# A fused mixer and MLP on one core: the first two input tiles alone, v's weights on another queue, and a new order of the steps

## The chip, the cores and the metric

The kernel runs on one core of one Trainium2 chip. A core has five engines that run their own instruction streams and meet at semaphores: TensorE (matrix products, PE in the profile, with PEld for its weight loads), VectorE (DVE), ScalarE (ACT), GpSimd (POOL) and SyncE (SP), which here only issues DMAs. The metric is the time of one execution in microseconds (us), median of three runs.

## The reference

`A_x` is 2048 rows of 512 numbers, all inputs are bfloat16.

```python
x  = A_x                                   # [1, 2048, 512]
xn = layernorm(x)                          # no learned scale or bias
# A: attention over 8 earlier positions, 2 apart; 32 heads of 16
q, k, v = split(xn @ wqkv)                 # wqkv [512, 1536]
logits  = sum_d q[s] * k[s - 2*u], u = 0..7, / 4; -1e9 where s < 2*u
s  = (softmax(logits) weighted sum of v[s - 2*u]) @ wo
# B: two MLP halves with shifts along the rows
h  = gelu(layernorm(xn) @ w1)
hs = concat(h's four quarters, shifted by +1, -1, +2, -2 rows) @ w2
x1 = xn + hs
g  = silu(x1 + gelu(layernorm(x1) @ w3) @ w4)   # w3 [512, 1376]
out = x + s * g
```

## The kernel before

The 2048 rows are worked on in four chunks of 512 rows (`c` 0 to 3), each of four tiles of 128 rows (`i` 0 to 15, in pairs `k` 0 to 7). The program is a list of small steps, `ORDER`, written out in a string. Each word of it is a step with its arguments: `qk.0.3.2` is step `qk` for chunk 0, column block 3, into PSUM bank 2. A step issues one to thirty-odd instructions on one engine. Each engine takes its instructions in the order of the list and waits at semaphores for what it reads, so the list sets the order on every engine at once, but not the times. Letters in a DMA step name the issuing queue: `s` SyncE, `a` ScalarE, `g` GpSimd.

The head of the list. `ldxp` (L221) loads a pair of x tiles, `ldv` (L234) half of v's weights (two of the four row blocks of the contraction), `ldw1` (L241) half of w1, `ldqk` (L228) the weights of q or k; all on SyncE's queue. `c_warm` (L275) clears a tile on VectorE, and `warmup` (L321) multiplies it with itself on TensorE, ten times 512 columns wide and later eight times 128 wide, while nothing else is there to do. `c_zero` (L288 to 290) writes 14 rows of zeros ahead of v in DRAM and clears the halo of `hT`, on GpSimd. For chunk 0, `st` (L333, L334) takes mean and variance on VectorE, `sq0` (L338) the square root on ScalarE, `nm0` (L344, L345) normalises on VectorE, `tr0` (L356) transposes on TensorE and `ev0h` or `ev0a` (L364, L360) moves the transposed tile to SBUF on ScalarE. For later chunks `xT` does it with a transposing DMA.

The matrix steps on TensorE: `v` (L471), `w1` (L496), `qk` (L443), `w2` (L611), `w3` (L668), `w4` (L685) and `wo` (L768); each takes four matmuls of 512 columns, `w4` eleven. `lg` (L543) sums products of q and k over a head, `ws` (L729) sums weighted v. Six PSUM banks (0 to 5) take the results, and a double one those of `lg`; the last argument of a step is its bank, and a bank is free again when ScalarE or VectorE has read it. ScalarE evicts `ev` (v, L481), `eqk` (L452), `eh` (gelu of w1, L507), `eg` (gelu of w3, L677). VectorE does `pw` (products of q and shifted k, L530), `smx`, `sms`, `smn` (softmax), `xa` (adds w2's result, L618), `st3s` (statistics of x1, L622), `nm3` (normalises x1, L645), `vp` (weights times v, L716), `ya`, `sg`.

DMAs in the middle: `sv` (L489, GpSimd) stores an evicted v tile to DRAM, out of a ring of three buffers `vt`; `vl` (L710, SyncE) reads v back with the shifts; `x1Tr` (L655), `hTr`, `oTr`, `tE` are transposing DMAs on SyncE. `x1Tr(k)` gives half a chunk of x1 transposed, which `w3` reads. `pre` copies x to the output, and `soa` (L835, GpSimd) adds a finished tile to it.

The tail: for tiles 12 to 15, `oTp` (L756) transposes on TensorE and `eoT` (L762) evicts; `wo` follows, then `ge` (L782), `gb` (L786), `fav` (L819) finish a tile; tile 15 goes in two halves, `woh`, `sgh`, `favh`, `soh`.

Of the kernel before, what the change touches and what calls it, by code (L numbers as in the profile page):

```python
# [9 lines left out]
ALU = mybir.AluOpType  # L10
# [18 lines left out]
qk.1.6.3 xa.1 nb.7 qk.1.0.2 nb.6 st3s.1 eqk.1.6 hTr.3 rr.4 xa.0 ldw3.s.0 st3s.0 eqk.1.5 pw.0.6
nm.13 nm.12 nm.15 qk.1.7.0 qk.1.3.4 w2.2.5 w1.9.3 w1.8.1 eh.9 eh.8 xa.2 rr.7 hTr.4 rr.5 rq.0  # L30
w1.10.5 pw.0.7 r3.0 v.8.3 eh.10 st3s.2 nm.14 w2.3.1 nm3.0 nm3.1 eqk.1.3 w2.5.5 ev.8 qk.2.0.4
xa.3 st3s.3 eqk.1.7 eqk.1.0 xT.6 lg.0.3 rq.1 kh.2 xa.5 lg.0.2 r3.1 w2.4.2 smx.0 ldw3.s.1 sv.8
xT.7 x1Tr.0 v.10.5 qk.2.4.0 w2.6.1 eqk.2.4 nm3.3 xa.4 ex.0 w2.7.3 w1.11.2 xa.6 st3s.6 nm3.2 xa.7
qk.2.5.1 eqk.2.0 x1Tr.1 eh.11 ev.10 sv.10 rr.6 v.9.0 v.11.3 w1.13.4 eqk.2.5 ev.9 hTr.5 qk.2.7.2
w1.15.1 eqk.2.7 w1.12.0 vl.s.2.0 vl.s.0.0 ldw4.s.2 qk.2.2.2 vl.s.3.1 eh.12 pw.1.0 st3s.4 st3s.7
st3s.5 v.12.5 eqk.2.2 pw.1.3 sms.0 eh.13 v.13.0 w3.0.6.4 ev.11 hTr.6 rq.2 qk.2.1.3 pw.1.2 r3.2
sv.9 eg.0.6 eqk.2.1 ldwo.s.3 smn.0 rq.3 pw.1.1 r3.3 w3.0.1.2 qk.2.3.4 w3.0.10.3 nm3.4 eqk.2.3
tE.0 eh.15 eg.0.10 ev.13 eg.0.1 lg.1.1 lg.1.0 pw.1.7 w2.8.1 w1.14.0 w3.0.0.2 eh.14 w3.0.2.3
hTr.7 qk.2.6.0 eqk.2.6 eg.0.0 w2.10.4 nm3.6 vl.s.0.1 nm3.7 x1Tr.3 vl.s.1.0 pw.1.5 xa.8 pw.1.4
nm3.5 pw.1.6 w2.11.1 xa.10 w3.0.8.2 xa.11 qk.3.1.4 st3s.11 eg.0.8 ev.12 w2.14.1 lg.1.2 st3s.10  # L40
sv.12 lg.1.3 eqk.3.1 w2.12.4 sv.11 st3s.8 eg.0.2 smx.1 w2.9.3 ldw4.s.1 x1Tr.2 xa.9 w2.15.5 xa.14
w3.0.3.2 w3.0.9.3 xa.12 pw.2.2 qk.3.2.1 qk.3.0.4 w2.13.0 st3s.9 eqk.3.2 eqk.3.0 eg.0.3 vl.s.9.1
ldw4.s.0 rq.4 xa.15 vl.s.9.0 vl.s.3.0 ldwo.s.2 pre.s.2 qk.3.3.1 w3.0.5.2 st3s.12 qk.3.4.5 eg.0.5
pw.2.3 eqk.3.3 qk.3.5.4 st3s.14 pw.2.4 xa.13 pw.2.1 rq.5 st3s.15 v.15.1 eqk.3.5 v.14.2 ev.15
eqk.3.4 w3.1.1.0 w3.0.4.5 vp.0 st3s.13 rq.6 pw.2.0 r3.4 nm3.9 w3.0.7.1 eg.0.4 ev.14 eg.0.9
eg.0.7 ex.1 qk.3.7.4 w3.1.0.2 eg.1.0 sv.14 r3.5 nm3.10 rq.7 nm3.11 x1Tr.5 w3.1.8.1 vl.s.2.1
# [27 lines left out]
def kernel(  # L74
# [116 lines left out]
    def xtile(i):  # L191
        return x_c[i // TPC][:, i % TPC, :]
# [71 lines left out]
    def ldwo(q, a):  # L264
# [5 lines left out]
        qs[q].dma_start(out=wo_sb[32 * a : 32 * a + 32, :, :], in_=src)  # L270


    @step
    def c_warm():
        nc.vector.memset(warm[:], 0.0)  # L275

    @step
    def c_ident():
        make_identity(nc, ident[:])

    @step
    def c_small():
# [1 line left out]
        nc.gpsimd.memset(mhalf[:], -0.5)  # L284

    @step
    def c_zero():
        nc.gpsimd.dma_start(out=v_dram[0:PADK, :], in_=warm[0:PADK, :])  # L288
# [586 lines left out]
```

## Time and profile before

| what | value |
|---|---|
| median of 3 runs | 190.42 us (190.27 to 190.52) |
| the profiled execution | 190.75 us |
| its span, first to last instruction | 189.0 us |
| TensorE busy | 182.8 us, 97% |
| VectorE busy | 165.1 us, 87% |
| ScalarE busy | 112.8 us, 60% |
| GpSimd busy | 42.7 us, 23% |
| granted TensorE clock, mean | 0.996 |
| DMA | 39.25 MB, mean 208 GB/s |

The profile is of one execution. Rows of the time line read: start, duration, engine, line of the kernel, operation, what it writes `<-` what it reads, how often, and in brackets how long the engine had been idle and what ended that. `SPq` and `ACTq` rows are the issuing of a DMA, not its transfer. The chain of waits follows back from the last instruction, at each step to what released it.

### The profile page before, as it was taken

How to read it: one execution, taken by the hardware profiler on the slowest of the kernel's cores; microseconds unless marked ns; L12 is line 12 of the kernel's file. 1: busy time of each engine (PE TensorE's matmuls, PEld its weight loads, DVE VectorE, ACT ScalarE, POOL GpSimd, SP SyncE). 2: the span in 40 equal slices, each digit the busy share in tenths (PEclk: the TensorE clock that was granted, in tenths of full speed). 3: DMA queues.
4: the chain of work that ended last, by engine and by line, in shares of the span. 5: the costliest groups of instructions: out<-in, count | busy, mean ns of one | idle time of the engine just before them, and what ended most of it. 6: DMA issues, size and time to landing. Idle time of an engine off the chain costs nothing.

```text
span 189.0 us, 3685 instructions
## 1 busy us (share of the span) xinstructions
PE 182.8 (97%) x1430; PEld 87.0 (46%) x1430; DVE 165.1 (87%) x270; ACT 112.8 (60%) x189; POOL 42.7 (23%) x70
## 2 busy tenths in 40 slices
PE   7999999999999999999999999999999999999990
PEld 2444445445444545444444555444455444444450
DVE  2694797997999899999989998999999999989554
ACT  3578669666595636045941465969529664742780
POOL 4157156423010702010450000000050003005350
PEclk9999999999999999999999999999999999999998
DMA  5994986987969929965989929999974999796783
GB/s 164 315 352 115 199 248 141 194 238 137 233 120 286 278 64 224 222 87 190 399 162 361 274 57 134 254 401 277 189 190 95 254 335 238 210 254 106 88 106 116
DMA packets 47842, 39.25 MB, mean 208 GB/s; under 512 B 35251, under 2 KB 41889, under 8 KB 47777
## 3 DMA queue, kind: packets, MB, share of 16 engines
q1 hardware_dynamic: 45008, 35.14, 74.6%
q0 software_dynamic: 2528, 3.69, 10.9%
q8 instruction: 11, 0.18, 0.4%
q10 hardware_dynamic: 288, 0.20, 0.3%
q14 instruction: 7, 0.05, 0.1%
HBM read 26.41 MB, written 5.78 MB: 170 GB/s over the span
## 4 chain that ended last, share of the span: by engine, by line
PE 85%; DMA 4%; DVE 4%; issue 2%; POOL 2%; SPq 1%; ACT 1%; POOLq 0%
PE mm L668 20%; PE mm L685 18%; PE mm L443 15%; PE mm L611 8%; PE mm L496 7%; PE mm L471 6%; PE lg L543 4%; PE mm L768 4%; DMA xc<-in_A_x_dram 3%; PE mm L729 3%; POOL out_dram L835 2%; DMA out_dram<-xr 1%; DVE st L333 1%; DVE xr L775 1%; DVE xr L786 1%
## 5 line engine op out<-in xcount | busy, mean ns | idle before, releaser
L530 DVE TENSOR_TENSOR pw<-qT,kT 128x2048 bf16<-128x2048 bf16 x32 | 38.3, 1214 | 3.4 <-PE lg L543 2.4
L668 PE MATMUL mm<-x1T,w_sb 128*128 128x512 bf16 (+1 forms) x176 | 40.9, 379 | 0.0
L685 PE MATMUL mm<-w_sb,h 128*128 128x512 bf16 (+1 forms) x176 | 39.4, 379 | 0.0
L677 ACT ACTIVATE h<-mm 128x512 bf16<-128x512 f32 (+1 forms) x44 | 23.9, 602 | 23.3 <-PE mm L668 17.6
L716 DVE TENSOR_TENSOR vs<-vs,att 128x4096 bf16<-128x4096 bf16 x16 | 36.2, 2285 | 0.0
L443 PE MATMUL mm<-xnT,wqk_sb 128*128 128x512 bf16 x128 | 30.6, 379 | 0.0
L835 POOL DMA_DIRECT2D out_dram<-xr x12 | 11.0, 1117 | 74.0 <-DVE xr L775 74.0
L668 PEld LDWEIGHTS <-w_sb 128*128 128x128 bf16 (+1 forms) x176 | 17.6, 100 | 20.4
L685 PEld LDWEIGHTS <-h 128*128 128x128 bf16 (+1 forms) x176 | 16.9, 98 | 20.8 <-issue 0.4
L443 PEld LDWEIGHTS <-wqk_sb 128*128 128x128 bf16 x128 | 12.4, 98 | 15.0
L452 ACT ACTIVATE kT<-mm 128x512 bf16<-128x512 f32 x16 | 9.4, 601 | 12.1 <-PE mm L443 11.9
L489 POOL DMA_DIRECT2D v_dram<-vt x16 | 9.6, 601 | 30.6 <-ACT vt L481 27.2
L471 PE MATMUL mm<-w2v_sb,xnT 128*128 128x512 bf16 x64 | 15.8, 379 | 0.0
L496 PE MATMUL mm<-w_sb,xnT 128*128 128x512 bf16 x64 | 15.8, 379 | 0.0
L611 PE MATMUL mm<-w2v_sb,hT 128*128 128x512 bf16 x64 | 15.7, 380 | 0.0
L768 PE MATMUL mm<-wo_sb,oT 128*128 128x512 bf16 x60 | 14.3, 379 | 0.0
L333 DVE BATCH_NORM_STATS2 st<-xc 128x6 f32<-128x512 bf16 x16 | 10.8, 676 | 3.9 <-DMA xc<-in_A_x_dram 3.9
L452 ACT ACTIVATE qT<-mm 128x512 bf16<-128x512 f32 x16 | 9.4, 605 | 7.8 <-PE mm L443 7.7
L635 POOL TENSOR_TENSOR rstd<-nmr,mhalf 128x2 f32<-128x2 f32 x8 | 9.1, 1136 | 19.8 <-DVE nmr L628 19.7
L507 ACT ACTIVATE ht<-mm,rs 128x512 bf16<-128x512 f32 x16 | 10.6, 690 | 4.4 <-PE mm L496 2.3
L696 ACT ACTIVATE xr<-xr 128x512 bf16<-128x512 bf16 x16 | 9.6, 630 | 6.0 <-DVE xr L692 6.0
L692 DVE TENSOR_TENSOR xr<-mm,xr 128x512 bf16<-128x512 f32 x16 | 10.6, 683 | 1.1 <-PE mm L685 0.9
(79 smaller groups left out, 218.5 us busy)
## 6 DMA issues: line engine op xcount, KB each, us to landing
vs<-v_dram SPq DMA_DIRECT2D x32, 512.0 KB, 5.8
v_dram<-vt POOLq DMA_DIRECT2D x16, 128.0 KB, 3.8
out_dram<-in_A_x_dram SPq DMA_DIRECT2D x3, 512.0 KB, 6.5
out_dram<-xr POOLq DMA_DIRECT2D x12, 128.0 KB, 3.5
w_sb<-in_B_w_dram SPq DMA_DIRECT2D x2, 688.0 KB, 4.9
w_sb<-in_B_w_dram SPq DMA_DIRECT2D x2, 640.0 KB, 6.8
xc<-in_A_x_dram SPq DMA_DIRECT2D x4, 256.0 KB, 5.9
wqk_sb<-in_A_wqkv_dram SPq DMA_DIRECT2D x2, 512.0 KB, 7.8
```

The source lines that it names most:

```text
L443: nc.tensor.matmul(pt, lhsT=wqk_sb[:, dt, nt * P : (nt + 1) * P], rhs=xnT[c][:, :, dt, :], start=(dt == 0), stop=(dt == ND - 1),)
L452: nc.scalar.activation(dst.rearrange("p (n i) -> p n i", i=TPC), mm.pop(("qk", c, nt)).rearrange("p (i n) -> p n i", i=TPC), AF.Copy,)
L471: nc.tensor.matmul(pt, lhsT=xnT[c][:, jj, dt, :], rhs=wv_sb[:, dt, :], start=(dt == 0), stop=(dt == ND - 1),)
L496: nc.tensor.matmul(pt, lhsT=xnT[c][:, jj, dt, :], rhs=w1_sb[:, dt, :], start=(dt == 0), stop=(dt == ND - 1),)
L530: nc.vector.tensor_tensor(out=pw_t[c, u], in0=q_t[c], in1=k_t[c][:, :, DIL * u : DIL * u + CH], op=ALU.mult)
L611: nc.tensor.matmul(pt, lhsT=hT[:, plane, g, p0 : p0 + P], rhs=w2_sb[:, g, :], start=(g == 0), stop=(g == ND - 1),)
L668: nc.tensor.matmul(pt[:fs, :], lhsT=w3_sb[:, dt, ft * P : ft * P + fs], rhs=x1T[c][:, :, dt, :], start=(dt == 0), stop=(dt == ND - 1),)
L677: nc.scalar.activation(h3[c, ft][:fs, :], mm.pop(("w3", c, ft))[:fs, :], AF.Gelu_apprx_tanh)
L685: nc.tensor.matmul(pt, lhsT=h3[c, ft][:fs, jj * P : (jj + 1) * P], rhs=w4_sb[:fs, ft, :], start=(ft == 0), stop=(ft == NF - 1),)
L716: nc.vector.tensor_tensor(out=vv, in0=vv, in1=att[c][:, :, H * jj : H * jj + H].unsqueeze(2).to_broadcast([P, NB * 2, DH, H]), op=ALU.mult,)
L768: nc.tensor.matmul(pt, lhsT=oT[i // 2][:, i % 2, dt, :], rhs=wo_sb[:, dt, :], start=(dt == 0), stop=(dt == ND - 1),)
L835: nc.gpsimd.dma_start(out=rows(out2, i), in_=xr[i], accum_op=ALU.add)
```

## The change

Four edits and a new list. Two x tiles are loaded each by a DMA of its own (`ldx`), first on SyncE's queue; the other pairs stay pairs. The two halves of v's weights are issued from ScalarE; `c_warm` clears one element of that weight tile on VectorE, so that ScalarE's issue waits for VectorE. `c_zero` is split: the zero rows (`c_zero.g`) and the halo (`c_halo`) have places of their own later in the list. The unused step `fag` goes, and `preh` comes in, which the list doesn't use. The steps are otherwise the same (three of the small warm-up matmuls fewer), in another order. In the changed file the lines are 11 to 15 further down.

```diff
 ORDER = """
-ldxp.s.0 c_warm c_small warmup.10.512.0 sqw c_ident kh.0 ldv.s.0 ldv.s.1 ldxp.s.1 ldw1.s.0
-ldw1.s.1 c_zero st.0 ldxp.s.2 ldxp.s.3 st.1 sq0.0 ldqk.s.0 ldqk.s.1 nm0.0 sq0.1 rp.0 nm0.1
-tr0.0.0 warmup.8.128.1 ev0h.0.0 ev0h.0.1 st.2 tr0.1.2 v.0.1 st.3 ev0h.1.0 ev0h.1.1 sq0.2 v.1.2
-ev.0 nm0.2 sq0.3 rp.1 w1.0.0 ev.1 nm0.3 rs.0 sv.0 st.5 tr0.2.1 ldxc.s.2 w1.1.2 ev0a.2 sv.1 rr.0
-st.4 tr0.3.3 rs.1 v.2.1 ev0a.3 st.7 rp.2 rs.2 w1.2.4 ev.2 st.6 eh.0 v.3.3 sv.2 rp.3 rr.1 w1.3.1
...
-oTp.13.4 soa.9 sg.10 oTp.14.3
-eoT.13 oTp.12.0 wo.11.5 eoT.12 oTp.15.4 eoT.14 wo.13.0 eoT.15 wo.14.3 wo.12.4 woh.15.0.1
-woh.15.1.2 soa.10 sg.11 soa.11 ge.13 gb.13 ge.14 fav.13 gb.14 so.s.13 ge.12 fav.14 gb.12 so.s.14
-sgh.15.0 fav.12 favh.15.0 so.a.12 sgh.15.1 soh.s.15.0 favh.15.1 soh.a.15.1
+ldx.s.0 c_warm c_small ldx.s.1 kh.0 warmup.10.512.0 ldv.a.0 c_ident ldv.a.1 sqw st.0 st.1 sq0.0
+nm0.0 sq0.1 nm0.1 tr0.0.1 warmup.5.128.0 ev0h.0.0 tr0.1.2 ev0h.0.1 v.0.0 ldxp.s.1 c_sel ldw1.s.0
+ldw1.s.1 ldxp.s.2 ldqk.s.0 ldxp.s.3 ldqk.s.1 rp.0 st.2 rs.0 ev0h.1.0 st.3 ev0h.1.1 sq0.2 v.1.1
+rr.0 sq0.3 nm0.2 w1.0.2 rp.1 nm0.3 ev.1 ev.0 sv.0 rs.1 st.5 ldxc.s.2 tr0.2.3 tr0.3.1 w1.1.0 ev0a.2
...
+qk.2.1.1 st3s.2
+w2.4.4 eqk.2.1 nm.14 qk.2.7.0 lg.0.2 ev.8 lg.0.3 xT.7 w1.10.2 nm3.1 rr.7 eqk.1.7 sv.8 nm3.0
+st3s.3 rq.1 xa.5 xa.4 smx.0 r3.1 w1.11.4 vl.s.2.1 x1Tr.0 eh.11 eh.10 hTr.5 w2.7.3 w2.6.5 st3s.5
+ex.0 v.11.2 xa.7 w1.13.4 v.10.3 st3s.4 rq.2 nm3.3 xa.6 v.15.1 ev.10 nm3.2 st3s.6 ev.11 x1Tr.1
+v.12.5 eh.13 c_zero.g w1.14.2 r3.2 sv.11 vl.s.3.1 pw.1.0 w1.12.3 eqk.2.7 v.14.4 st3s.7 eh.12
+ev.12 w2.8.0 hTr.6 nm3.4 rq.3 eh.14 r3.3 w1.15.5 sv.12 sv.10 w3.0.2.2 eh.15 ev.14 hTr.7 w3.0.5.3
+qk.2.5.4 nm3.5 pw.1.1 xa.8 sms.0 eqk.2.5 x1Tr.2 qk.2.4.5 w3.0.7.0 eqk.2.4 eg.0.5 pw.1.2 nm3.6
...
+wo.8.3 sg.9 si.14 eo.15 oTp.13.5 soa.9 sg.8 oTp.12.0 wo.14.1 eoT.13 eoT.12 soa.8 wo.13.5 ge.14
+gb.14 ge.13 fav.14 gb.13 so.s.14 fav.13 oTp.15.0 wo.12.1 eoT.15 ge.12 woh.15.0.0 woh.15.1.5
+so.s.13 sgh.15.0 gb.12 favh.15.0 sgh.15.1 soh.s.15.0 fav.12 favh.15.1 so.a.12 soh.a.15.1
 """
...
     @step
+    def ldx(q, i):
+        if 0 not in x_c:
+            x_c[0] = rot("xc", 0, 2, [P, TPC, D])
+        qs[q].dma_start(out=xtile(i), in_=rows(x2, i))
+
+    @step
...
     def c_warm():
         nc.vector.memset(warm[:], 0.0)
 
+        nc.vector.memset(wv_sb[0:1, 0, 0:1], 0.0)
+
...
     @step
-    def c_zero():
-        nc.gpsimd.dma_start(out=v_dram[0:PADK, :], in_=warm[0:PADK, :])
+    def c_zero(q):
+        qs[q].dma_start(out=v_dram[0:PADK, :], in_=warm[0:PADK, :])
+
+    @step
+    def c_halo():
         nc.gpsimd.memset(hT[:, :, :, 0:HALO], 0.0)
         nc.gpsimd.memset(hT[:, :, :, HALO + S // TPC :], 0.0)
```

More of the change, by code (lines that the diff above doesn't have):

```diff
@@ L29 @@
[L29 to L34, printed above, removed]
@@ new lines @@
+sv.15 eqk.2.6 eqk.2.0 st3s.13 pre.s.2 lg.1.0 rq.7 rq.5 vl.s.1.1 vl.s.1.0 vl.s.9.0 vl.s.3.0
+pre.s.1 rq.4 r3.7 lg.1.1 pw.1.6 w3.0.4.1 r3.4 pw.1.7 w3.1.7.0 kh.2 qk.2.2.4 pw.1.5 w3.0.3.3
+eqk.2.2 st3s.12 w3.0.1.5 eg.0.4 vp.2 nm3.8 eg.0.3 qk.3.5.1 eg.0.1 lg.1.3 lg.1.2 w4.0.5 pw.2.4
+rq.6 smx.1 r3.6 r3.5 kh.3 qk.3.7.3 w4.1.4 sv.14 sv.13 pw.2.0 ex.1 ya.0 w4.3.2 eqk.3.7 eqk.3.5
+nm3.9 ya.1 vp.3 ldwo.s.1 vl.s.0.1 x1Tr.4 vl.s.0.0 qk.3.2.1 sms.1 nm3.10 ya.3 w4.2.3 eqk.3.2
+nm3.11 x1Tr.5 qk.3.3.1 qk.3.6.4 eqk.3.6 vl.s.9.1 w3.1.0.2 eqk.3.3 eg.1.7 qk.3.0.5 w3.1.1.1
@@ L831, in pre, with preh, half @@
         )
+    @step
+    def preh(q):
+        def half(t):
+            return t[(NCH - 1) * CH :, :].rearrange("(p i) d -> p (i d)", i=TPC)[:, 0 : 2 * D]
+        qs[q].dma_start(out=half(out2), in_=half(x2))
     @step
```

77 lines of the change are left out of this document (35 added, 42 removed).

## The prediction, made before the changed kernel was run

> **What bounds the kernel now.** I read the page's busy times first, then what TensorE waited for, then stretches of the run, then the chain of waits. The page (busy us, share of the span):
>
> ```profile
> span 189.0 us, 3685 instructions
> PE 182.8 (97%) x1430; PEld 87.0 (46%) x1430; DVE 165.1 (87%) x270; ACT 112.8 (60%) x189; POOL 42.7 (23%) x70
> ```
>
> TensorE is busy 97% of the span. Its own waits, in full (engine, line, released by: us, times, longest):
>
> ```profile
> PE mm L321 <- DVE warm L275: 1.2, 1, 1.2
> PE mm L356 <- DVE xr L345: 0.5, 2, 0.3
> ```
>
> Both stand at the head. Stretches (us of the stretch, then busy us of each engine, clock, DMA share, GB/s):
>
> ```profile
> 1.18:7.06 5.88, 5.63 (x27) 2.54 (x27) 2.65 (x9) 2.17 (x6) 2.31 (x6) 1.00 0.73 232
> 7.06:10.11 3.05, 2.80 (x15) 1.07 (x13) 2.15 (x8) 2.08 (x7) 0.22 (x1) 1.00 1.06 379
> 10.11:184.55 174.44, 174.41 (x1392) 83.38 (x1392) 158.30 (x249) 108.09 (x178) 39.62 (x57) 1.00 0.88 208
> 184.55:189.00 4.45, 0.00 (x0) 0.00 (x0) 1.71 (x6) 0.00 (x0) 0.00 (x0) 0.82 0.35 114
> ```
>
> From 10.11 to 184.55 us TensorE is idle for 0.03 us. That stretch does the same matmuls after the change, so nothing can be won in it and anything can be lost. What can be won lies ahead of 10.11 and behind 184.55. The chain of waits at the head (start, us, what):
>
> ```profile
> 2.15 5.68 DMA xc<-in_A_x_dram
> ...
> 7.85 0.71 DVE st L333
> ...
> 10.11 0.40 PE mm L356 x4
> ...
> 22.03 0.86 PE mm L496 x4
> ```
>
> Issued at 2.15, the second pair of x tiles lands at 7.83, and 2.28 us of statistics and normalising later the third transpose can start. The last row is the price of one step of four matmuls: 0.86 us. The head in order of time:
>
> ```profile
> 0.73 0.40 SPq L221 DMA_DIRECT2D xc<-in_A_x_dram  x1
> 0.85 0.27 DVE L275 MEMSET warm<- 128x256 uint32 x1 [0.85 <-PEq L859]
> 1.18 4.45 PE L321 MATMUL mm<-warm 128*128 128x512 bf16 x10 [1.18 <-DVE warm L275]
> 1.18 0.93 SPq L234 DMA_DIRECT2D w2v_sb<-in_A_wqkv_dram  x2
> 1.50 0.73 POOL L288 DMA_DIRECT2D v_dram<-warm  x1
> 3.61 0.69 DVE L333 BATCH_NORM_STATS2 st<-xc 128x6 f32<-128x512 bf16 x1 [2.49 <-DMA xc<-in_A_x_dram]
> 4.56 0.30 ACT L338 ACTIVATE ve<-mv,eps_t 128x1 f32<-128x1 f32 x1 [2.34 <-DVE mv L334]
> 5.87 0.61 PE L356 MATMUL mm<-ident,xr 128*128 128x128 bf16 x4 [0.24 <-DVE xr L345]
> 6.27 0.72 PE L321 MATMUL mm<-warm 128*128 128x128 bf16 x8
> 6.52 1.40 ACT L364 ACTIVATE xnT<-mm 128x256 bf16<-128x256 bf16 x4 [0.86 <-PE mm L356]
> 6.83 0.39 PE L356 MATMUL mm<-ident,xr 128*128 128x128 bf16 x4
> 7.06 1.94 PE L471 MATMUL mm<-w2v_sb,xnT 128*128 128x512 bf16 x8
> 8.83 1.03 PE L496 MATMUL mm<-w_sb,xnT 128*128 128x512 bf16 x4
> 9.64 0.41 DVE L345 TENSOR_SCALAR xr<-xc,mv,rs 128x512 bf16<-128x512 bf16 x1
> 10.23 0.41 DVE L345 TENSOR_SCALAR xr<-xc,mv,rs 128x512 bf16<-128x512 bf16 x1
> ```
>
> Real work (v of tile 0) starts at 7.06; three steps, 2.59 us at 0.86 each, fill 3.05 us. So the head wastes 0.46 us behind 7.06 and, ahead of it, what an earlier first tile could save.
>
> **The change, part by part.** *First tile alone.* Two tiles (256 KB) landed by 3.61. At the 379 GB/s of 7.06:10.11 one tile less is 0.35 us less, so tile 0 lands at about 3.25 (bounds: 3.61, if the fixed part is all; 2.5, which is its issue at 0.73 plus the shortest 128 KB transfer of the page, below).
>
> ```profile
> out_dram<-xr SPq DMA_DIRECT2D x2, 128.0 KB, 1.8
> ```
>
> From the statistics (3.61) to the first transpose (5.87) is 2.26 us; 3.25 + 2.26 = 5.5. The ten warm-up matmuls still run from 1.18 for 4.45 us, so the transposes cannot start before 5.45 to 5.63. I take 5.55: 0.32 won, and no more can be won here even if the tile lands at 2.5.
>
> *Five small warm-ups for eight.* The eight took 0.72 us; three fewer save 0.27 at that mean. From first transpose to v were 7.06 - 5.87 = 1.19 us; now 0.92 if they ran as fast. They start earlier, though, where matmuls are slow: four transposes took 0.61 us at 5.87 and 0.39 at 6.83. I add 0.25 for that: v starts near 5.55 + 1.2 = 6.75 (bounds: 6.55, the eviction, which began 0.65 behind the transpose and takes 1.40 / 4 = 0.35; and 7.06, nothing won).
>
> *v's weights on ScalarE's queue, behind one element cleared on VectorE.* The extra memset costs VectorE under 0.1 us while it waits for x anyway. ScalarE issues near 1.25, two issues in 0.93 us, and only then loads its first table. Behind them stand that load (1.28 us, about 2.2 to 3.5), the square root that warms it and the first real one, which came at 4.56 and would come at 4.2: hidden, with 0.5 us to spare; beyond that it delays the first transpose one for one. SyncE's queue loses these 0.93 us, so the second x pair is issued near 1.65 instead of 2.15. Its landing is the open term. From both sides: 7.83, if v's bytes take the same share of the engines in front of it; or much earlier, because v's second half was itself late:
>
> ```profile
> DMA to landing us min/median/max: 3.1/4.3/5.5
> ```
>
> (the two loads of line 234.) The second took 2.4 us longer than the first, where 256 KB at 379 GB/s are 0.7; 1.7 us are lost there and passed on to x. If that loss belonged to the zeroing DMA of line 288, which was issued at 1.50, it goes with it, and x lands near 5.4. If the two queues share evenly, 768 KB are ahead of x's end instead of 1 MB: 0.7 us less, 7.1. I take 7.0, nearest to the sharing case.
>
> The Trainium skill (DMA: Bandwidth & Descriptors, Rules for kernel authors) says that spreading DMAs over issuing engines gives no bandwidth, since all use the same 16 engines and interleave; it only saves issue time. By that rule alone x lands at 7.1, and the gain below is 0.5 instead of 0.65.
>
> *The third and fourth transposes* now stand together behind w1 of tile 0: 6.75 + 2.59 = 9.34 instead of 10.11, if x landed by 9.34 - 2.28 = 7.06. The fourth is normalised 0.59 later (9.64 and 10.23 above), while the transposes are only 0.4 or less apart, so it may wait 0.1 to 0.35. Won so far: 0.77, less 0.1 = 0.65 (0 to 0.95).
>
> *Zeroing the pad rows and hT's halo later, sel earlier.* On GpSimd, busy 23%. The halo (before w2) and the pad rows (before v is read back for tile 0, more than thirty steps on) have ample lead; sel runs before 3 us, while GpSimd would wait for the first statistics. Nothing; if sel ran over, rs.0 and then rr.0 would be later, on DVE alone.
>
> *The new list behind the head.* Same steps, so TensorE's 174.4 us stay. SyncE's queue now issues w3's second half before its first, the first copy of x to the output and the w4 loads earlier, moves two wo loads and reorders the reads of v; GpSimd's adds to the output change order with them. Each load has ten or more steps of 0.86 us until its first reader, and without that lead costs what it is late. Two fewer table loads on ScalarE, which is busy 60%: nothing. The places with little lead are rivals, below.
>
> *The tail.* Only one step of wo (0.86) now stands between the transpose of tile 15 and the first half product woh that needs its eviction; before, there were three. ScalarE has the copy of wo 13 to finish and then that eviction:
>
> ```profile
> 180.90 1.09 ACT L762 ACTIVATE oT<-mm 128x512 bf16<-128x512 bf16 x2 [0.22 <-PE mm L768]
> 182.85 0.60 ACT L782 ACTIVATE vt<-mm 128x512 bf16<-128x512 f32 x1 [0.27 <-PE mm L768]
> ```
>
> 0.60 + 0.55 + about 0.1 of hand-over against 0.86 + 0.2: woh waits 0.2 us. In return two tiles' multiplies and adds are off VectorE before woh, some 0.3 us of its last chain. I take 0 (-0.3 to +0.3).
>
> **Sum.** -0.65 us against the profiled execution's 190.75 gives 190.1. That execution is 0.33 above the median of 190.42; the forecast median is 189.8 (own range 189.1 to 190.4).
>
> **Rivals.** *A: x1T comes late (slower).* For w3 of chunk 0 the second transposing DMA, x1Tr.1, follows nm3.2. On VectorE nm3.2 now comes behind softmax 0 (mean ns before the last bar):
>
> ```profile
> 46.80 0.83 DVE L556 MEMSET lg<- 32x14 f32 x7 [0.40 <-PE lg L543]
> 47.67 1.23 DVE L558 TENSOR_REDUCE mx<-lg 128x128 f32<-128x1024 f32 x1
> 48.93 1.23 DVE L561 TENSOR_TENSOR lg<-lg,mx 128x1024 f32<-128x1024 f32 x1
> ...
> 50.39 1.28 DVE L618 TENSOR_TENSOR xr<-mm,xr 128x512 bf16<-128x512 f32 x2
> 51.70 0.69 DVE L622 BATCH_NORM_STATS2 st<-xr 128x6 f32<-128x512 bf16 x1
> ```
>
> Behind the last lg of chunk 0: 0.83 + 1.23 + 1.23, two statistics of 0.69 + 0.17, two adds of 0.69, and three small steps of 0.17 to 0.4: 7.3 us. TensorE has 14 steps until w3 needs it: 12.0 us. That leaves 4.7 us from issue to landing. The eight x1T transfers took:
>
> ```profile
> DMA to landing us min/median/max: 3.0/5.8/12.1
> ```
>
> At the median w3 waits 1.1 us, and the run ends at 190.9; at the longest 7.4, near 197. It decides from 5.35 us on. For it: the median. Against it: few transfers are queued ahead here. Chance 0.20.
>
> *B: v's store comes late (slower).* Only three vt buffers exist: the eviction of v 14 waits for the store of v 11, and qk.2.5 waits for that eviction's bank, ten steps (8.6 us) behind v 11. The store is issued some 3 us behind v 11 and the eviction takes 0.6, so 5.0 us are left; stores took
>
> ```profile
> DMA to landing us min/median/max: 2.1/3.8/10.5
> ```
>
> At 10.5 the wait is 5.5, less 0.65: 195.3; at 7.15, half way from 3.8 to 10.5, it is 2.15: 191.9. It decides from 5.65 us on, where the wait eats the 0.65. Chance 0.10.
>
> *C: the head gives nothing (same).* Sharing makes x land at 7.83 again or v's second half late; the third transpose stays at 10.1: 190.4. Chance 0.10. *D: the matmuls speed up later than now* (between 6.27 and 6.83, by the rows above). If at 8.0, the 1.25 us from 6.75 do half their work and 0.62 is lost again: 190.4. Chance 0.03; the three runs of before lie within 0.25 us, which speaks against a wandering switch. The Trainium skill (TensorE: Matmul & The Clock Gate, What's actually happening) calls the window free-running, so the switch may vary by run; one trace cannot show that.
>
> **How the numbers follow.** Forecast 0.57, A 0.20, B 0.10, C 0.10, D 0.03. 0.2% is 0.38 us, about what a measurement here can tell. Forecast is faster, A and B slower, C and D the same: 0.57, 0.30, 0.13. The range runs from 189.1 (0.95 won at the head, 0.3 at the tail) to 192.1, which takes in C, D, A near its median and half of B.
>
> **What would show it.** Right: the first transpose near 5.5, v near 6.75, the third transpose near 9.4, no zeroing DMA at the head, v's second half landing in under 4.5 us, and then TensorE idle by less than 0.3 us up to woh, with its end 0.6 earlier. Wrong: a TensorE gap ahead of w3.0.2 or qk.2.5 (lines 679 and 454 of the new file), or x's second pair still landing near 7.8.

## The result

The changed kernel takes 190.36 us in the median of 22 runs (189.93 to 190.97); the kernel before, run on the same chips, 189.86 us (22 runs, 189.71 to 190.52). The ratio is 1.0022, 95% interval 1.0013 to 1.0031: slower, by just over what can be told from no change. Forecast were 189.8 us and faster, with 0.30 on slower; the range of 189.1 to 192.1 holds the time, but neither of the two slower rivals is what happened.

The 190.42 us of the three runs shown before were high: the same kernel gave 189.86 to 190.04 in every later comparison. The forecast median of 189.8 was 0.62 below the first figure and is level with the second.

The profiled execution of the changed kernel took 190.40 us, its span 188.3. The top of its page (busy us, share of the span, instructions; of the 1427 matmuls that go with the weight loads 15 records are missing):

```profile
span 188.3 us, 3667 instructions
PE 180.7 (96%) x1412; PEld 86.3 (46%) x1427; DVE 164.3 (87%) x271; ACT 110.0 (58%) x187; POOL 40.5 (21%) x70
```

What TensorE waited for, in full (engine, line, released by: us, times, longest):

```profile
PE mm L332 <- DVE w2v_sb L283: 1.2, 1, 1.2
PE mm L367 <- DVE xr L356: 1.1, 1, 1.1
PE mm L696 <- issue: 0.2, 1, 0.2
```

There is no wait of w3 (line 679) or qk (line 454) here: rivals A and B did not happen. The third line, 0.2 us "issue" at line 696, stands where matmul records are missing. Stretches of the changed kernel (us of the stretch, busy us of each engine, clock, DMA share, GB/s):

```profile
1.20:6.81 5.61, 4.54 (x23) 1.94 (x24) 3.10 (x10) 2.51 (x6) 1.05 (x4) 1.00 0.79 261
6.81:9.20 2.39, 2.39 (x13) 1.08 (x13) 2.25 (x10) 1.69 (x6) 0.46 (x1) 1.00 1.06 375
182.91:188.30 5.39, 1.05 (x8) 0.70 (x8) 2.21 (x7) 0.55 (x1) 0.00 (x0) 1.00 0.42 116
```

Between 6.81 us, the start of v, and 9.20, where the third transpose begins with its weight load, TensorE is busy without a gap; in the profile of before this stretch was 3.05 us with 0.25 idle. (Where nothing waits, a weight load starts some 0.21 us ahead of its first matmul, here 9.20 and 9.41; in the profile of before both started at 10.11. Counted to the matmul the stretch is 2.60 us against 3.05.) The last eight matmuls (`woh`) run from 182.91 for 1.05 us, so TensorE ends at 183.96, against 184.55 in the profile of before. By the traces the changed kernel looks 0.7 us faster (span 188.3 against 189.0); by the runs it is 0.5 us slower. Both differences have their own cause, below: the profile of before shows an unusual execution, and part of the time of the changed kernel lies outside the span.

The head of the changed kernel in order of time (start, us, engine, line, operation, in brackets the idle time and its end; rows of the small steps are left out):

```profile
0.74 0.87 SPq L212 DMA_DIRECT2D xc<-in_A_x_dram  x2
...
1.20 0.97 ACTq L240 DMA_DIRECT2D w2v_sb<-in_A_wqkv_dram  x2
1.20 3.67 PE L332 MATMUL mm<-warm 128*128 128x512 bf16 x10 [1.20 <-DVE w2v_sb L283]
...
3.17 0.69 DVE L344 BATCH_NORM_STATS2 st<-xc 128x6 f32<-128x512 bf16 x1 [2.03 <-DMA xc<-in_A_x_dram]
...
4.47 0.69 DVE L344 BATCH_NORM_STATS2 st<-xc 128x6 f32<-128x512 bf16 x1 [0.40 <-DMA xc<-in_A_x_dram]
...
5.47 0.41 DVE L356 TENSOR_SCALAR xr<-xc,mv,rs 128x512 bf16<-128x512 bf16 x1
...
5.94 0.40 PE L367 MATMUL mm<-ident,xr 128*128 128x128 bf16 x4 [1.07 <-DVE xr L356]
...
6.81 1.90 PE L482 MATMUL mm<-w2v_sb,xnT 128*128 128x512 bf16 x8
...
9.20 0.65 PEld L367 LDWEIGHTS <-xr 128*128 128x128 bf16 x8
...
9.41 0.61 PE L367 MATMUL mm<-ident,xr 128*128 128x128 bf16 x8
```

The first tile came at 3.17, earlier than forecast (3.25), and nothing came of it: the list puts the second tile's statistics ahead of the first tile's normalising on VectorE, the second tile came only at 4.47, and the normalising (5.47) and the first transpose (5.94) followed from there. In brackets TensorE waits 1.07 us for it. The tail:

```profile
181.78 0.60 ACT L793 ACTIVATE vt<-mm 128x512 bf16<-128x512 f32 x1 [0.27 <-PE mm L779]
...
182.27 0.59 ACT L773 ACTIVATE oT<-mm 128x512 bf16<-128x512 bf16 x1
...
182.91 0.77 PEld L804 LDWEIGHTS <-oT 128*128 128x128 bf16 x8 [0.58 <-ACT oT L773]
...
185.10 0.29 DVE L818 TENSOR_TENSOR xr<-xc,xr 128x256 bf16<-128x256 bf16 x1
185.22 0.37 ACTq L854 DMA_DIRECT2D out_dram<-xr  x1
185.71 0.37 ACTq L824 DMA_DIRECT2D out_dram<-xr  x1
```

The last step of wo began at 181.80 and its four matmuls are 0.86 us, so `woh` could have started at 182.66; it started at 182.91, released by ScalarE's eviction: a wait of 0.25 us (forecast 0.2). The list of waits above doesn't have it, since it gives those four matmuls 1.03 us, up to 182.83. The last store is issued at 185.71, 0.32 us behind VectorE's last instruction (185.39).

### The profile page after: what moved, and what is told of

It is laid out like the page before. It is cut to its first block, busy times and chain, and to the rows that moved or that the text cites. A ratio compares the mean times of both kernels' runs of the same rounds, so it can differ in the third digit from the quotient of the medians.

```text
span 188.3 us, 3667 instructions
## 1 busy us (share of the span) xinstructions
PE 180.7 (96%) x1412; PEld 86.3 (46%) x1427; DVE 164.3 (87%) x271; ACT 110.0 (58%) x187; POOL 40.5 (21%) x70
## 4 chain that ended last, share of the span: by engine, by line
PE 93%; DMA 2%; DVE 2%; issue 1%; ACT 0%; SPq 0%; DVEq 0%
PE mm L679 20%; PE mm L696 20%; PE mm L454 15%; PE mm L507 7%; PE mm L482 7%; PE mm L622 7%; PE mm L779 6%; PE lg L554 4%; PE mm L740 4%; DMA xc<-in_A_x_dram 2%; PE mm L367 1%; PE mm L767 0%; DVE xr L813 0%; DVE st L344 0%; PE mm L804 0%
## 5 line engine op out<-in xcount | busy, mean ns | idle before, releaser
L454 PE MATMUL mm<-xnT,wqk_sb 128*128 128x512 bf16 x128 | 31.1, 379 | 0.1
L622 PE MATMUL mm<-w2v_sb,hT 128*128 128x512 bf16 x60 | 14.9, 380 | 0.1
L754 ACT ACTIVATE o<-mm 128x512 bf16<-128x512 f32 x16 | 9.0, 594 | 7.6 <-issue 6.9
L646 POOL TENSOR_TENSOR rstd<-nmr,mhalf 128x2 f32<-128x2 f32 x8 | 7.6, 961 | 22.5 <-DVE nmr L639 22.5
```

The source lines that it names most:

```text
L454: nc.tensor.matmul(pt, lhsT=wqk_sb[:, dt, nt * P : (nt + 1) * P], rhs=xnT[c][:, :, dt, :], start=(dt == 0), stop=(dt == ND - 1),)
L622: nc.tensor.matmul(pt, lhsT=hT[:, plane, g, p0 : p0 + P], rhs=w2_sb[:, g, :], start=(g == 0), stop=(g == ND - 1),)
```

## The experiments

In each table and text, "outside" is a run's time minus its span (the span is given to 0.1 us, so a single value is good to 0.05). "VectorE" is the number of instructions in VectorE's compiled program, waits included. None of these kernels leaves out work. Medians:

| kernel | VectorE | us | ratio to before, 95% | span | outside |
|---|---|---|---|---|---|
| before (in the five comparisons) | 306 | 189.93 to 190.04 | | 188.2 to 188.3 | 1.76 to 1.79 |
| changed | 313 | 190.36 | 1.0013 to 1.0031 | 188.25 | 2.12 |
| before, built again | 306 | 189.86 | 0.9983 to 1.0006 | 188.1 | 1.75 |
| old list, zeroing late | 306 | 190.12 | 0.9989 to 1.0013 | 188.35 | 1.78 |
| new head, old list | 307 | 189.92 | 0.9978 to 1.0002 | 188.1 | 1.76 |
| old head, new list | 312 | 190.55 | 1.0013 to 1.0042 | 188.6 | 2.01 |
| before, v's weights by ScalarE | 307 | 190.94 | 1.0031 to 1.0056 | 189.15 | 1.79 |
| new head, first tile first | 307 | 190.73 | 1.0022 to 1.0067 | 188.95 | 1.78 |
| changed, tail by bank 3 | 313 | 190.68 | 1.0017 to 1.0044 | 188.55 | 2.10 |

### Which part costs: the head or the list

*Before, built again*, is the kernel before without an edit, to have a second trace of it. *Zeroing late* moves the zeroing DMA away from the head:

```diff
-ldw1.s.1 c_zero st.0 ...
+ldw1.s.1 c_halo st.0 ...
-w2.4.2 smx.0 ldw3.s.1 ...
+w2.4.2 smx.0 c_zero.g ldw3.s.1 ...
```

> The kernel before, profiled once more. Theory 1 (the profile that the prediction was read from was an unusually slow execution: its 190.75 us lies above all 22 timed runs of that kernel, 189.71 to 190.52): time 189.9, span near 188.1, and at the head the second load of v's weights lands in under 4.5 us instead of 5.5 and the third transpose starts before 9.9 instead of 10.11. Theory 2 (the head is always so, and the two kernels differ in what lies outside the span: 1.75 us there, 2.1 in the changed kernel): span 188.1 or not, the head looks as before, third transpose at 10.0 to 10.2. Ratio 1.000 in both.

> The kernel before with one change: the DMA that zeroes the pad rows leaves the head and is issued behind softmax 0; the halo is cleared where it was. If that DMA makes v's second half and x's second pair late (theory of the prediction): they land in 4.0 and 4.6 us, third transpose 0.4 earlier, time -0.4 us. If it does not: no change, within 0.1 us, and the last of v's parts is as late as before.

Built again the kernel gives 189.86 us, and its trace has v's second half at 4.98 us and the second pair of tiles at 6.80. Without the zeroing DMA at the head they landed at 5.87 and 7.12, no earlier, and the time is the same. With it, in the other traces of the old head, v's second half landed anywhere from 4.98 to 7.17, so no run shows that this DMA delays anything.

*New head, old list* takes the changed kernel's loads, v's weights on ScalarE, the late zeroing and the five warm-ups, and keeps the old list behind them; *old head, new list* the reverse (the clearing of the halo and `sel` stay with their list).

```diff
-ldxp.s.0 c_warm c_small warmup.10.512.0 sqw c_ident kh.0 ldv.s.0 ldv.s.1 ldxp.s.1 ...
+ldx.s.0 c_warm c_small ldx.s.1 kh.0 warmup.10.512.0 ldv.a.0 c_ident ldv.a.1 sqw ldxp.s.1 ...
```

> The kernel before with the whole new head (two single x tiles, v's weights on ScalarE's queue, zeroing DMA later, five small warm-ups) and the old list behind it. Prediction's reading: -0.6 us against before. Theory 1: -0.3 to 0, since the usual head wastes less. Theory 2: the span falls by 0.3 to 0.6 but the time by 0.35 less than the span, if what is outside the span belongs to the new head.

> The changed kernel's list behind the old head (x in pairs, v's weights and all loads on SyncE's queue in the old order, zeroing DMA at the head, eight small warm-ups). If the new list costs what the head wins (theory 3): +0.5 us or more against before, with TensorE gaps behind 12 us. If the list is neutral, as predicted: within 0.2 us of before. Theory 2 with the outside part belonging to the list: time minus span 2.1 us.

The head alone makes no difference (0.9978 to 1.0002); the list alone makes the kernel slower by as much as the whole change does. The head of the kernel before, built again, in order of time:

```profile
2.15 0.47 SPq L221 DMA_DIRECT2D xc<-in_A_x_dram  x1
...
3.50 0.69 DVE L333 BATCH_NORM_STATS2 st<-xc 128x6 f32<-128x512 bf16 x1 [2.38 <-DMA xc<-in_A_x_dram]
...
5.76 0.40 PE L356 MATMUL mm<-ident,xr 128*128 128x128 bf16 x4 [0.40 <-DVE xr L345]
...
6.66 1.93 PE L471 MATMUL mm<-w2v_sb,xnT 128*128 128x512 bf16 x8
6.82 0.69 DVE L333 BATCH_NORM_STATS2 st<-xc 128x6 f32<-128x512 bf16 x1 [0.53 <-DMA xc<-in_A_x_dram]
...
9.08 0.42 PEld L356 LDWEIGHTS <-xr 128*128 128x128 bf16 x4
...
9.29 0.39 PE L356 MATMUL mm<-ident,xr 128*128 128x128 bf16 x4
```

The third tile comes at 6.82, not at 7.85 as in the profile the forecast was made from, and the third transpose at 9.08, not 10.11, with the zeroing DMA at the head as ever. v to third transpose is 2.42 us (2.63 to its matmul), with no gap. Over the traces of this study, the third transpose taken by its weight load:

| | v starts at | third transpose behind it | TensorE's end behind it |
|---|---|---|---|
| profile of before | 7.06 | 3.05 | 177.49 |
| old head, old list, eight other traces | 6.58 to 7.36 | 2.41 to 2.43 | 176.97 to 176.99 |
| old head, old list, zeroing late | 6.67 | 2.72 | 177.17 |
| new head, old list | 6.62 | 2.39 | 176.95 |
| old head, new list | 7.35 | 2.37 | 177.15 |
| changed, and five variants of it | 6.36 to 7.20 | 2.38 to 2.39 | 177.07 to 177.39 |

(The eight are the kernel before built again and the seven kernels with more clears at the head, below.) TensorE's program from v on takes the same time to 0.02 us whenever the third transpose is not late, and it was late in two traces of ten with the old head and list. The gap of the forecast belongs to single executions. Where v starts moves by 0.8 us from execution to execution, with either head. The new list costs 0.17 us up to TensorE's end (177.15 against 176.98): the wait of `woh`, 0.25, less a remainder of 0.08 that was not followed up. Up to the span's end it costs only 0.09: from v on 181.40 us in each of the eight to 0.01, 181.49 in the changed kernel.

### The head's parts: v's weights on ScalarE's queue, and the first tile

*v's weights by ScalarE* does that one part in the old kernel; the first two tiles stay one transfer.

```diff
-ldxp.s.0 c_warm c_small warmup.10.512.0 sqw c_ident kh.0 ldv.s.0 ldv.s.1 ldxp.s.1 ...
+ldxp.s.0 c_warm c_small warmup.10.512.0 ldv.a.0 ldv.a.1 sqw c_ident kh.0 ldxp.s.1 ...
```

> The kernel before with v's weights alone moved to ScalarE's queue, behind the clear on VectorE; the first two tiles stay one transfer, the zeroing stays at the head. VectorE has 307 instructions. By the prediction's sharing case the second pair of tiles lands near 7.0 where v's weights shared SyncE's queue with it; in an ordinary execution of the kernel before it lands at 6.8. Theory 'the order of bytes is all, the queues share one set of engines': the second pair, now issued at 1.65 instead of 2.15, lands 0.4 to 1.2 earlier, at 5.6 to 6.4, and v's second half as much later, at 5.6 to 6.4 instead of 4.98; v of tile 0 still starts at 6.6 to 6.8, as TensorE waits for the tiles' chain there, and the third transpose gains up to 0.3. Time 189.9 +- 0.2, the same. Rival: v waits for its weights (a gap of over 0.2 us in front of it or inside it), 190.2 or more.

The rival is what came, with a gap of 0.68 us. Waits of TensorE and two rows of the time line:

```profile
PE mm L480 <- DMA w2v_sb<-in_A_wqkv_dram: 0.7, 1, 0.7
```

```profile
6.90 0.59 PE L480 MATMUL mm<-w2v_sb,xnT 128*128 128x512 bf16 x2
...
8.18 1.46 PE L480 MATMUL mm<-w2v_sb,xnT 128*128 128x512 bf16 x6 [0.68 <-DMA w2v_sb<-in_A_wqkv_dram]
```

The second pair of tiles did land early, at 4.99. But v's second half, issued at 1.66, landed at 8.13; with the old head it landed at 4.98 to 7.17. Between that issue and that landing SyncE's queue, with the pair and w1, moved 1.38 MB, and ScalarE's, with v's weights, 0.52 MB. v stands still after two matmuls, and the kernel loses 1.0 us. In the changed kernel that half landed at 7.13, close to where v's third matmul needed it (6.81 + 0.43 = 7.24). So the two queues shared the engines, as the forecast's sharing case had it, but what came later was v's weights. The Trainium skill (DMA: Bandwidth & Descriptors, Rules for kernel authors) says that spreading DMAs over issuing engines gives no bandwidth; these landings agree.

*First tile first* keeps the new head and puts the first tile's normalising ahead of the second tile's statistics, v and w1 of tile 0 ahead of those of tile 1, and eight long warm-ups for ten:

```diff
-st.0 ldxp.s.2 ldxp.s.3 st.1 sq0.0 ldqk.s.0 ldqk.s.1 nm0.0 sq0.1 rp.0 nm0.1 tr0.0.0
+st.0 ldxp.s.2 ldxp.s.3 sq0.0 ldqk.s.0 ldqk.s.1 nm0.0 st.1 sq0.1 rp.0 nm0.1 tr0.0.0
-... ev0h.0.0 ev0h.0.1 st.2 tr0.1.2 v.0.1 st.3 ev0h.1.0 ev0h.1.1 sq0.2 v.1.2 ev.0 nm0.2 sq0.3 rp.1 w1.0.0 ev.1
+... ev0h.0.0 ev0h.0.1 st.2 v.0.1 tr0.1.2 st.3 ev0h.1.0 ev0h.1.1 sq0.2 w1.0.0 v.1.2 ev.0 nm0.2 sq0.3 rp.1 ev.1
```

> The new head with the old list, and in it the first tile's normalising ahead of the second tile's statistics on VectorE, v and w1 of tile 0 ahead of those of tile 1, and eight long warm-up matmuls for ten. Theory 'the tile that lands early is wasted because its normalising stands behind the second tile's statistics': the first transpose comes at 5.0 to 5.2 instead of 5.73, v starts at 5.9 to 6.1 instead of 6.62, and the span shortens by 0.3 to 0.5 to 187.5 to 187.8, median 189.4 to 189.7. Rival 'the weights or the second pair of tiles are the bound': v or w1 waits for weights, which landed at 6.37 and 7.80, or the third transpose stays at 9.0 to 9.4 with TensorE idle in front of it, and the span stays within 0.15 of 188.1.

```profile
PE mm L505 <- ACT vt L490: 0.5, 1, 0.5
PE mm L365 <- DVE xr L354: 0.4, 1, 0.4
PE mm L480 <- ACT xnT L373: 0.4, 1, 0.4
```

The first half of the theory holds: the first transpose came at 5.16, where the changed kernel had 5.94, so the list was what wasted the early tile. The gain did not come: v still started at 6.57, behind the tile's evictions on ScalarE, and w1 of tile 1 waited 0.46 us for the eviction of v of tile 1, which my order had put right ahead of it in the same bank. That it lost is a matter of this order; whether another one gains is open.

### The wait in the tail

*Tail by bank 3* transposes and evicts tile 15 two steps of wo earlier, as the old list does.

```diff
-... sg.8 oTp.12.0 wo.14.1 eoT.13 eoT.12 soa.8 wo.13.5 ge.14 ... fav.13 oTp.15.0 wo.12.1 eoT.15 ge.12 woh.15.0.0
+... sg.8 oTp.12.0 oTp.15.3 wo.14.1 eoT.13 eoT.12 eoT.15 soa.8 wo.13.5 ge.14 ... fav.13 wo.12.1 ge.12 woh.15.0.0
```

> The changed kernel with tile 15 transposed and evicted two steps of wo earlier, as in the kernel before (the transpose goes to bank 3). The wait of the first half product for its eviction, 0.25 us in the changed kernel, goes: span 0.2 to 0.3 shorter than the changed kernel's 188.25. Theory 'outside goes with the tail's order': the time outside the span falls from 2.13 back towards 1.77, and the median to 189.8. Rival 'outside goes with something ahead of the tail': it stays at 2.0 to 2.15, and the median is 190.1.

```profile
PE mm L765 <- DVE xr L784: 0.3, 1, 0.3
```

The wait of `woh` went, and one of 0.34 us came: bank 3 was still being read by VectorE. The time outside stayed at 2.10, so it has nothing to do with this part of the tail. A second try with bank 2 (*both*, below) has neither wait, but its twelve transposes and the start of wo behind them take 0.86 us (179.78 to 180.64) where the eight and the four had taken 0.66, because ScalarE's eviction of tile 15's sums ends only near 180.35. From v to TensorE's end it is 177.07 against 177.16 in the same kernel without it: 0.1 us won of 0.25. VectorE and the stores behind that take 4.44 us instead of 4.34, though, so up to the span's end nothing is won (181.52 against 181.50). A span 0.2 to 0.3 shorter was expected; the median is 0.35 longer, 190.27 against 189.92. That is a miss, and these two traces, alike from v on, don't explain it.

### The time outside the span

Of the 0.50 us between the medians 0.36 lie outside the span, and they came with the new list, not with the head. The new list makes VectorE's program longer: a step that waits for a second engine needs a wait instruction of its own, and there are 37 of these instead of 31, and one more clear. First, the old kernel with three more clears on GpSimd, whose program had also grown, or with seven more on VectorE:

```diff
+        for _ in range(3):
+            nc.gpsimd.memset(eps_t[:], EPS)
```

```diff
         nc.vector.memset(warm[:], 0.0)
+        for _ in range(7):
+            nc.vector.memset(warm[0:1, 0:1], 0.0)
```

> The kernel before with three more tiny clears on GpSimd at its head (101 instructions there instead of 98, as many as the changed kernel has). Theory 'outside goes with an engine's instruction count', GpSimd's: the time outside the span, 1.77 us in the kernel before and 2.13 in the changed one, rises to 2.0 or more here and the median goes to 190.1 to 190.3. Rival 'outside goes with the order of the steps': it stays at 1.75 to 1.80 and the median at 189.9 +- 0.2.

> The kernel before with seven more one-element clears on VectorE at its head, behind the clearing of the warm-up tile (312 to 313 instructions there, as in the changed kernel, instead of 306). If VectorE's count sets the time outside the span, it rises from 1.77 to 2.0 or more. If not, it stays at 1.75 to 1.80. The seven clears cost the span nothing or up to 0.4 us (the first warm-up matmul waits for VectorE and then starts up to 0.4 us later, but the transposes start at 5.75 by what they wait for on VectorE, not by the warm-up).

| kernel | VectorE | us | ratio to before, 95% | span | outside |
|---|---|---|---|---|---|
| before, 3 clears on GpSimd | 306 | 190.05 | 0.9983 to 1.0012 | 188.3 | 1.78 |
| before, 7 clears of the warm-up tile | 313 | 190.90 | 1.0018 to 1.0057 | 188.8 | 2.12 |
| changed, six additions on GpSimd | 307 | 189.92 | 0.9980 to 1.0005 | 188.15 | 1.77 |
| the same and bank 2 (*both*) | 307 | 190.27 | 0.9986 to 1.0032 | 188.5 | 1.77 |
| before, 5 clears | 311 | 190.11 | 0.9991 to 1.0019 | 188.3 | 1.77 |
| before, 7 clears | 313 | 190.54 | 1.0003 to 1.0035 | 188.45 | 2.09 |
| changed, 4 clears | 317 | 190.58 | 1.0003 to 1.0040 | 188.5 | 2.05 (1.74 to 2.09) |
| before, 15 clears | 321 | 190.27 | 0.9997 to 1.0029 | 188.35 | 1.88 |
| before, 20 clears | 326 | 189.85 | 0.9979 to 1.0007 | 188.1 | 1.75 |
| changed, 14 clears | 327 | 190.11 | 0.9989 to 1.0016 | 188.35 | 1.79 |
| before, 23 clears | 329 | 190.10 | 0.9986 to 1.0020 | 188.3 | 1.79 |

(In the span of the kernel with seven clears of the warm-up tile stands a second loss: the warm-up waits for them and starts at 1.99 instead of 1.18, and the transposes, at 6.28, behind it.) VectorE's program it is. The test on the changed kernel itself moves six additions of a 128 by 2 tile to GpSimd:

```diff
-            nc.vector.tensor_scalar(
+            nc.gpsimd.tensor_scalar(
                 out=ve1[:, k, 0:2], in0=var, scalar1=EPS, scalar2=None, op0=ALU.add
             )
```

> The changed kernel with the six additions of EPS to the variance (step rp, for the second to last chunk) on GpSimd instead of VectorE: 307 instructions on VectorE instead of 313, nothing else moved. Theory 'the time outside the span goes with VectorE's instruction count': it falls from 2.13 us to 1.75 to 1.85 and the median with it, to 190.0 +- 0.2. Rival 'it goes with the order of the new list, and the padded kernel before had another reason': it stays at 2.05 to 2.15 and the median at 190.4. Both: the span stays at 188.25 +- 0.2, its first half product still waits 0.25.

> The same, and tile 15 transposed two steps of wo earlier into bank 2, whose last reader is the eviction of ws on ScalarE that the transpose waits for anyway. Theory: the first half product no longer waits, no wait comes in its place (bank 3 had one of 0.34 us on VectorE), the span is 0.2 to 0.3 shorter than that of the kernel without this, near 188.0, time outside 1.8, median 189.7 to 189.9: level with the kernel before. Rival: TensorE is held elsewhere in the tail, or VectorE's last chain sets the end, and the span does not move.

With six instructions fewer the changed kernel is level with the kernel before: 189.92 us, outside 1.77. But is it the count? Clears of a tile that nothing reads, 5 and 20 of them:

```diff
+        pad = sb.tile([1, 1], F32, name="pad", tag="pad")
+        for _ in range(5):
+            nc.vector.memset(pad[:], 0.0)
```

> The kernel before with five clears of a tile of its own on VectorE at the head, which nothing reads: 311 instructions. The first tile of x comes at 3.5, so they are hidden and the span stays at 188.2 +- 0.2. Time outside the span: 307 instructions gave 1.77, 312 gave 2.0, 313 gave 2.12. If it is a step in the count, it is 1.77 or 2.1; if it grows by each instruction from some count on, it is 1.9 to 2.0.

> The kernel before with twenty such clears: 326 instructions on VectorE. They take some 1.2 us of VectorE's 2.4 us of waiting at the head and stay hidden; span 188.2 +- 0.2. Time outside the span: if it grows by some 0.07 us with each instruction, 3 us; if it is a step, 2.1 to 2.2.

Twenty more cost nothing, against both forms of the theory as I had stated it. So the place at which the program ends was tried, with 7, 15 and 23 clears, and 4 in the changed kernel:

> The kernel before with seven clears of a tile of its own on VectorE at the head: 313 instructions. So far 306, 307, 311 and 326 gave 1.75 to 1.79 us outside the span, 312 gave 2.0, 313 gave 2.1 (the changed kernel, its variant with another tail, and the kernel before with seven clears of the warm-up tile). Theory 'the time outside goes with the place at which VectorE's program ends': 2.1 us here, median 190.3. Rival 'not the count, but what the added instructions were (the warm-up tile that TensorE waits for; the waits of the new list)': 1.77, median 189.95. Span 188.2 +- 0.2 by both.

> Fifteen such clears: 321 instructions. If the place counts with a period of eight instructions (312 and 313 are long, 320 and 321 would be), 2.1 us outside the span; with a period of 16 or 32, or no period, 1.77. Span 188.2 +- 0.2.

> Twenty-three such clears: 329 instructions. With a period of eight or 16, 2.1 us outside the span; with 32 or none, 1.77. Span 188.2 +- 0.2.

> The changed kernel with four more clears on VectorE at the head, which nothing reads: 317 instructions, nothing taken away. Theory 'the place at which VectorE's program ends': with four instructions MORE the time outside the span falls from 2.13 to 1.77 and the median from 190.36 to 190.0, as it did with six fewer. Rival 'work of the six waits themselves': it stays at 2.1 or grows. Span 188.25 +- 0.2.

313 instructions give 2.1 us again, whatever the seven added ones are, so the count decides. A period of eight or 16 falls (329 is short, 321 between). Four more in the changed kernel did not mend it, a miss: 317 is still long, in nine of twelve runs 1.98 to 2.09 and in three 1.74 to 1.80. The long time stands in a window from 312 to some 321 instructions. Fourteen more in the changed kernel lead out of it on the far side:

> The changed kernel with fourteen more clears on VectorE at the head, which nothing reads: 327 instructions. By the counts so far (306 to 311: 1.75 to 1.79 us outside the span; 312: 2.0; 313: 2.1; 317: mostly 2.05, in a quarter of the runs 1.78; 321: 1.88; 326 and 329: 1.75 to 1.79) the time outside is long in a window from 312 to some 321 and short on both sides. Theory 'the window in VectorE's count is the whole cause': 1.75 to 1.8 here, and a median of 190.05 +- 0.15 against 190.36. Rival 'in the changed kernel the long time needs fewer instructions, more do not help': 2.05 to 2.15. Span 188.25 +- 0.2.

That held: 327 instructions, 1.79 us. For what the window may be, look at the DMA queues: the rows of the instruction queues (packets, MB, share of 16 engines) between 160 us and the end of the span; first the old kernel with 20 clears:

```profile
q8 instruction: 1, 0.02, 0.2%
q14 instruction: 1, 0.01, 0.1%
```

and the changed kernel (313):

```profile
q8 instruction: 1, 0.02, 0.3%
```

The kernels with 326, 327 and 329 instructions have one fetch more on the second queue, 8 KB at 176.7 to 178.6 us, while there is still work to do. Those with 307, 311, 313 and 317 have none there. The one with 321, whose span is 188.8 us, has it here, from 188.7 us on:

```profile
q14 instruction: 1, 0.01, 0.7%
```

It was issued at 189.8 us, after the last instruction of the span. That this queue's fetches go with VectorE's program, the old kernel with more clears shows: the first one behind the start comes at 22.3 us with 306 instructions, 20.6 with 311, 18.7 with 313, 14.2 with 321 and 13.5 with 326. So a longer program needs one more block of instructions; with some 326 it is fetched early and hidden, and with 321 behind the span. That with 312 to 317 the end also waits for such a fetch, issued later still, fits, but no record reaches that far; it is argued, not shown. The Trainium skill (Runtime: NRT & Kernel Launch, Instruction fetch mechanics) says that a sequencer fetches the next block by a DMA queue of its own while it executes the present one, in blocks of 16 KB; the first queue's 0.02 MB agree with that size, the second queue's blocks are 8192 bytes here.

## Why the prediction was wrong, point by point

- **What bounds the kernel**: right in that TensorE is the bound from v on and nothing can be won there. Wrong in "So the head wastes 0.46 us behind 7.06". This is the step that failed. It took a wait of one execution for a property of the kernel. The third tile was 1.0 us late in it (7.85 against 6.82), and in eight other traces of the old head and list the stretch is 2.42 us (2.63 to 2.64 counted to the matmul, as the forecast's 3.05 and 2.59 are), so that at most 0.05 of the 0.46 is left. The execution's 0.33 us above the median was noted and not followed up: the late tile was the candidate.
- **First tile alone**, 0.32: nothing. The tile landed even earlier than forecast. The step left out that its normalising stands behind the second tile's statistics on VectorE; that tile landed at 4.45 in the changed kernel, and at 3.92 to 4.84 in its variants. Where it landed at 3.92 (the variant with 14 clears) the first transpose came at 5.49 and v at 6.36, as forecast and better:

```profile
4.06 0.66 DVE L347 BATCH_NORM_STATS2 st<-xc 128x6 f32<-128x512 bf16 x1
...
5.49 0.40 PE L370 MATMUL mm<-ident,xr 128*128 128x128 bf16 x4
...
6.36 1.90 PE L485 MATMUL mm<-w2v_sb,xnT 128*128 128x512 bf16 x8
```

- **Five warm-ups for eight**, 0.27 with 0.25 taken back: v came 0.87 us behind the first transpose, forecast 1.2, in the old kernel built again 0.90. Nothing either way.
- **v's weights on ScalarE's queue**: the second pair of x landed at 6.41 (forecast 7.0, by sharing), but ordinary executions of before have 6.33 to 7.32. That the zeroing DMA made v's second half late is not borne out: with it at the head that half landed at 4.98 to 7.17, without it at 5.87 in the one trace that tests it alone. And v's half pays for x; alone, the move costs 1.0 us.
- **Third and fourth transposes** at 9.34: the matmuls came at 9.41, right, and worth nothing, since the old kernel built again has 9.29. The fourth did not wait (eight transposes in 0.61 us).
- **Zeroing and halo later, sel earlier**: nothing, right.
- **The new list behind the head**, "nothing": the second term that was mis-sized. TensorE's work is the same to 0.08 us, but a longer program on VectorE (six more waits, one more clear) brought 0.36 us outside the span, which the sum took as a constant (190.75 less 189.0, 1.75).
- **The tail**, 0 (-0.3 to +0.3): the wait of 0.25 was forecast as 0.2. VectorE's last chain, from TensorE's end to its own last instruction, won 0.32 as forecast: 1.43 us against 1.75 in the old kernel built again. What the sum left out is the last store: the new order puts tile 12's last add behind the first half of tile 15, so ScalarE's queue issues tile 12's store at 185.22 for 0.37 us, and tile 15's last store goes out at 185.71, 0.32 behind VectorE's end. In the old kernel built again that is 0.08:

```profile
185.10 0.29 DVE L807 TENSOR_TENSOR xr<-xc,xr 128x256 bf16<-128x256 bf16 x1
185.47 0.34 ACTq L813 DMA_DIRECT2D out_dram<-xr  x1
```

So of the 0.32 only 0.08 is left, and against the 0.17 up to TensorE's end the new list costs 0.09 in the span.
- **Rivals**: A and B did not happen. C is what the head did, though not for its reasons; I gave it 0.10. D, a later switch of the matmul rate, was too low at 0.03: the ten warm-ups took 3.67 us in the changed kernel's trace and 4.45 in that of before, and with the old head and the new list eight small ones ran slow from 6.16 on:

```profile
6.16 1.06 PE L329 MATMUL mm<-warm 128*128 128x128 bf16 x8
...
7.35 1.89 PE L479 MATMUL mm<-w2v_sb,xnT 128*128 128x512 bf16 x8
```

That is 1.06 us where the profile of before has 0.72, and v starts at 7.35. So the switch wanders, for both kernels: by the spacing of the matmuls' starts (427 ns before it and 216 after at 512 columns, 107 and 56 at 128) it came near 4.0 us in the changed kernel's trace, and with the old head and the new list near 7.2. The Trainium skill (TensorE: Matmul & The Clock Gate, What's actually happening) calls its window free-running, with half a microsecond to either side; the traces show a wider spread, and no row shows the cause.

The sum as the runs have it: head 0 (-0.08 between medians, within its spread), list up to TensorE's end +0.17, behind it -0.08, outside +0.36, together +0.45, and measured +0.50; the rest is less than the start of v moves from execution to execution.

## What to carry to other kernels

Before a stall at the head of a profile is priced, take a second trace of the same kernel: here one DMA that was late by 1 us in one execution was the whole of the forecast gain (the forecast third transpose, 9.34, is where an ordinary execution of before has it). A tile that lands earlier is worth something only if the engine's list lets the next step run before it waits for the following tile. And compare a run's time with its span: a reordering that only adds waits can lengthen an engine's program, and here that cost 0.36 us that no row of the span shows; six instructions off that engine, or fourteen on, took it back.

## What the hardware showed that was not expected

- The time outside the span depends on the length of VectorE's program: 1.75 to 1.79 us with 306 to 311 and 326 to 329 instructions, 2.0 to 2.12 with 312 to 317, 1.88 with 321.
- At a given length, 317, it took either of two values, 1.74 to 1.80 or 1.98 to 2.09 us, from run to run.
- Two heads that differ by five hidden clears gave starts of v that lie 0.8 us apart (6.58 and 7.36): the first tile landed at 3.39 and 3.57, and the matmuls sped up near 4.4 and 7.2.
- Two queues do not keep the order of issue: v's second half, issued by ScalarE at 1.66 us, landed at 8.13, and 256 KB of w1, issued by SyncE at 1.64 behind the pair of tiles, at 7.89; with all loads on SyncE's queue the same half, issued at 1.64, landed at 4.98 to 7.17 in ten traces.
